# Stage 2's gate and value projections as seven products of quarters, with split weight quarters streamed from DRAM

## The chip, the core and the metric

The kernel runs on one core of one Trainium2 chip. The metric is device time in microseconds of one execution. The profile is one execution taken by the hardware profiler; it has its own time beside that of the runs.

## The reference

Three parts in a row, all in float32, over 2304 tokens (4 batches of 576) and a width of 512 (8 heads of 64):

```
attn = softmax(mask(q @ k.T / 8)) @ v          # window of 32; half of the heads with dilation 4
x1   = attn as (2304, 512)
x2   = ((x1 @ w1) * (x1 @ w2)) @ w3 @ w_out    # inner width 1024
out  = (silu(x2 @ w_gate) * (x2 @ w_val)) @ w_out2    # inner width 1536
```

## The kernel before

Everything is transposed: features lie on the 128 partitions and tokens along the free axis. The host only lays the inputs out. Weights come as 64-bit floats in blocks of two 128 x 512 pieces (`w_in`, 1 MB each), in the order of `W_ORDER` (lines 48 to 58).

A float32 product is made of three TensorE matmuls (`mm3`, lines 182 to 187): each operand is kept as a high part, rounded to the type `float32r`, and a low part, the rest, and high x high, high x low and low x high are summed in PSUM. `to_parts` (line 133) splits an operand: ScalarE copies it to the high part, VectorE subtracts. `convert_weights` (line 152) does it for a weight block: ScalarE and VectorE make a float32 of the 64-bit value (lines 166 to 170), ScalarE copies the high part (172), GpSimd subtracts (173).

Blocks of weights and of tokens pass through two or three staging buffers `raw`, in the order of the list `blocks` (line 95): `load_block` issues the DMA on SyncE's queue, `next_block` converts, `done_with` gives the buffer back and loads the next.

Stage 1 (lines 454 to 510) handles the tokens in four chunks of 512 and one of 256. For each of 8 inner blocks k it projects with `w1` (`gate_a`, 12 matmuls into bank `ba`), with `w2` (`gate_b`, 12 into `bb`), multiplies the two, splits the product `p`, and one block later contracts it with `w3 @ w_out`, made earlier on the chip (`contract`, 12 matmuls into four banks). The attention of the next batches runs between the blocks of chunks 0 to 2. In chunk 3 six of stage 2's weight blocks are converted, in chunk 4 nine.

Stage 2 (lines 513 to 537) does the same with 12 inner blocks, `Silu` on the gate, and all its weights resident in SBUF. Its x comes back from DRAM (`x2d`) a chunk at a time.

The program's order on each engine's queue is not the written one: the tile framework plans it from a timing model of its own, by readiness and the written order as priority. `tc.issue_after` ties instructions behind another on its engine.

Of the kernel before, what the change touches and what calls it, by code (L numbers as in the profile page):

```python
# [53 lines left out]
for _k in range(K2):  # L54
    W_ORDER.append((("wg", _k), ("wv", _k)))
    if _k % 2 == 0:
        W_ORDER.append((("wo2", _k), ("wo2", _k + 1)))
# [9 lines left out]
SPLIT_1 = {3: [1, 1, 1, 1, 1, 1, 0, 0], 4: [1, 1, 1, 1, 1, 1, 1, 2]}  # L67
SPLIT_2 = [1, 1, 1, 1, 0, 0, 0, 0, 0, 0, 0, 0]


def moe_chain_kernel(tc, q_in, k_in, v_in, w_in, mask_in, out):
# [8 lines left out]
    with static as st, other as ot, psum as pp, dram as dp:  # L80

        wslot = [st.tile([P, 2, 2, 512], F32R, name=f"w{i}") for i in range(12)]
        xb = [st.tile([P, 2, KT, CMAX], F32R, name=f"x{i}") for i in range(2)]
        pr = st.tile([P, 2, 2, CMAX], F32R, name="p")
        ta = st.tile([P, CMAX], F32, name="ta")
        raw = [ot.tile([P, 2, 512, 2], U32, name=f"raw{i}") for i in range(2)]
# [4 lines left out]
        x2d = dp.tile([KT, P, NT], F32, name="x2d")  # L91
        count = {"att": 0, "p": 0, "o": 0}


        blocks = [("w", i) for i in range(N_W1)] + [("x1", c) for c in (1, 2, 3)]
        blocks += [("w", i) for i in range(N_W1, N_W1 + 6)] + [("x1", 4)]
        blocks += [("w", i) for i in range(N_W1 + 6, N_W1 + 10)] + [("x2", 0)]
        blocks += [("w", i) for i in range(N_W1 + 10, NW)]
        blocks += [("x2", c) for c in range(1, NC)]
# [5 lines left out]

        def x_of(kind, c):
            return xb[(c + (NC if kind == "x2" else 0)) % 2]

        def load_block():
# [7 lines left out]
            if kind == "w":  # L117
                dst = r.rearrange("p (b f) -> p b f", b=2)
                src = w_in[i]
            else:  # L120
                a, size = CHUNKS[i]
                dst = r[:, :KT * size].rearrange("p (m t) -> p m t", m=KT)
                src = (x1d if kind == "x1" else x2d)[:, :, a:a + size].rearrange("m p t -> p m t")
# [3 lines left out]
        def done_with(n):  # L127

            if n < N_W1 or raw_at[n] is not raw[2]:
                raw_free.append(raw_at[n])  # L130
            load_block()
# [5 lines left out]
        def next_block():  # L137
# [5 lines left out]
            else:  # L143
# [3 lines left out]
                for m in range(0, KT, 2):  # L147
                    x = x_of(kind, i)[:, :, m:m + 2, :size]
                    to_parts(r[:, m:m + 2], x[:, 0], x[:, 1])
            done_with(n)  # L150

        def convert_weights(n, names):
# [10 lines left out]
            for b, w in slots:  # L163
                r = raw_at[n][:, b]
                lo, hi = r[:, :, :, 0], r[:, :, :, 1]
                nc.scalar.activation(hi.bitcast(F32), hi.bitcast(F32), AF.Prelu, scale=REBIAS, alpha=SIGN_UP)  # L166
                nc.vector.tensor_scalar(out=lo, in0=lo, scalar1=29, scalar2=None, op0=ALU.logical_shift_right)  # L167
                nc.vector.scalar_tensor_tensor(  # L168
                    out=lo, in0=hi, scalar=3, in1=lo, op0=ALU.logical_shift_left, op1=ALU.bitwise_or
                )  # L170
                x = lo.bitcast(F32)
                nc.scalar.activation(w[:, :, 0], x, AF.Copy)  # L172
                nc.gpsimd.tensor_tensor(out=w[:, :, 1], in0=x, in1=w[:, :, 0].bitcast(F32), op=ALU.subtract)  # L173

# [65 lines left out]
        with att1_pool as a1, att2_pool as a2:  # L240
# [5 lines left out]
            raw.append(a1.tile([P, 2, 512, 2], U32, name="raw2"))  # L246
            raw_free.extend(raw)
            xr = a1.tile([P, REST], F32, name="xr")
# [205 lines left out]
            def stage1(c, between, after):  # L454
                first, n = CHUNKS[c]
                x = x_of("x1", c)[:, :, :, :n]
# [19 lines left out]

            def rest(k):
# [13 lines left out]
        more1_pool = tc.tile_pool(name="more1", bufs=1, reuse_waits="tile")  # L491
        more2_pool = tc.tile_pool(name="more2", bufs=1, side="right", reuse_waits="tile")
        with more1_pool as m1, more2_pool as m2:
            assert not free and n_split[0] == N_W1 + 3
            free.extend([m1.tile([P, 2, 2, 512], F32R, name=f"wl{i}") for i in range(4)])
            free.extend([m2.tile([P, 2, 2, 512], F32R, name=f"wr{i}") for i in range(2)])

            def first_six(k):
                for _ in range(SPLIT_1[3][k]):
                    next_block_behind_p()  # L500
                if k == K1 - 1:
                    next_block()

            def replace(k):
                release(("w1", k), ("w2", k))
                for _ in range(SPLIT_1[4][k]):
                    next_block_behind_p()

            stage1(3, lambda n: None, first_six)
            stage1(4, lambda n: None, replace)  # L510


            for c, (first, n) in enumerate(CHUNKS):
                x = x_of("x2", c)[:, :, :, :n]
                for k in range(K2):
                    gate_a(("wg", k), x, n, AF.Silu)
                    p = gate_b(("wv", k), x, n)
                    flush()
                    if c == 0:
                        if k == 0:  # L520
# [83 lines left out]
```

## Time and profile before

| | us |
|---|---|
| three runs, median (lowest to highest) | 910.43 (908.68 to 911.29) |
| the profiled execution | 909.69 |
| its span, first to last instruction | 907.5 |
| TensorE busy | 881.4 |
| VectorE, ScalarE, GpSimd busy | 336.0, 312.3, 132.0 |

The profiled execution's time is 2.2 us more than its span; what lies outside is the start and the end of the program. Busy times of engines overlap, since engines run beside each other. A matmul's recorded time is its own latency, and the next one starts before it ends.

### The profile page before, as it was taken

To read this page: it belongs to the slowest core of one execution; us is meant where nothing else is said; L and a number is where in the kernel's file an instruction comes from. 1 tells how busy PE (TensorE), PEld (TensorE's weight loads), DVE (VectorE), ACT (ScalarE), POOL (GpSimd) and SP (SyncE) were. 2 spreads that over 40 slices of the span, in tenths; PEclk is the share of its full clock that TensorE was granted. 3 is DMA by queue.
4 is the path that set the end of the run, shared out by engine and by line. 5 is a ranking of instruction groups with operands and counts; after the bars stand their busy time and mean duration, and the time that the engine had idled before them with its cause. 6 is when DMAs were issued, how large, how long until landed. Compare 5 with 4: busy or idle time off the path is not lost.

```text
span 907.5 us, 11771 instructions
## 1 busy us (share of the span) xinstructions
PE 881.4 (97%) x4850; PEld 737.6 (81%) x4850; DVE 336.0 (37%) x487; ACT 312.3 (34%) x682; POOL 132.0 (15%) x83
## 2 busy tenths in 40 slices
PE   8889899989999999999999999999999999999998
PEld 5667688868888878889988888888888888888998
DVE  5887952333324213344766313111221112111221
ACT  4966743343525423343555212111221112111111
POOL 4656531000100100321343000000000000000000
PEclk8989899999999999999999999999999999999999
DMA  9786622332224113333555302000010001000100
GB/s 296 253 275 237 211 61 61 93 126 88 77 91 155 33 46 116 122 119 139 208 178 173 106 1 70 1 0 1 1 47 1 0 1 47 1 0 1 47 1 24
DMA packets 45909, 79.58 MB, mean 88 GB/s; under 512 B 3232, under 2 KB 29472, under 8 KB 41120
## 3 DMA queue, kind: packets, MB, share of 16 engines
q1 hardware_dynamic: 40096, 69.39, 23.5%
q10 hardware_dynamic: 5760, 9.44, 2.8%
q8 instruction: 38, 0.62, 0.3%
q14 instruction: 15, 0.12, 0.0%
HBM read 65.72 MB, written 13.11 MB: 87 GB/s over the span
## 4 chain that ended last, share of the span: by engine, by line
PE 83%; DVE 6%; DMA 4%; ACT 3%; issue 2%; POOL 1%; SPq 0%; DVEq 0%; POOLq 0%; ACTq 0%
PE bk L185 26%; PE bk L186 26%; PE bk L187 26%; PE bk L286 3%; DMA raw<-w_in 2%; DVE raw L168 2%; PE bk L338 2%; DVE raw L167 2%; PE bk L323 1%; POOL w L173 1%; ACT raw L166 1%; ACT s L305 1%; DMA q<-q_in 1%; ACT w L172 1%; DMA raw<-x1d 1%
## 5 line engine op out<-in xcount | busy, mean ns | idle before, releaser
L185 PE MATMUL bk<-x,w 128*128 128x512 f32 (+1 forms) x640 | 239.8, 375 | 3.2 <-ACT x L134 2.5
L186 PE MATMUL bk<-x,w 128*128 128x512 f32 (+1 forms) x640 | 238.5, 373 | 1.4 <-DVE x L135 1.4
L187 PE MATMUL bk<-x,w 128*128 128x512 f32 (+1 forms) x640 | 238.2, 372 | 0.0
L210 DVE TENSOR_TENSOR ta<-bk,ta 128x512 f32<-128x512 f32 (+1 forms) x100 | 63.7, 637 | 354.7 <-PE bk L187 323.7
L185 PEld LDWEIGHTS bk<-x,w 128*128 128x128 f32 x640 | 121.5, 190 | 23.5 <-ACT x L134 2.9
L186 PEld LDWEIGHTS bk<-x,w 128*128 128x128 f32 x640 | 121.6, 190 | 21.4 <-DVE x L135 2.4
L187 PEld LDWEIGHTS bk<-x,w 128*128 128x128 f32 x640 | 121.6, 190 | 19.8
L204 ACT ACTIVATE ta<-bk 128x512 f32<-128x512 f32 (+1 forms) x100 | 55.3, 553 | 227.2 <-PE bk L187 215.5
L186 PE MATMUL bk<-p,w 128*128 128x512 f32 (+1 forms) x320 | 118.5, 371 | 1.1 <-DVE p L135 1.1
L187 PE MATMUL bk<-p,w 128*128 128x512 f32 (+1 forms) x320 | 118.0, 370 | 0.0
L185 PE MATMUL bk<-p,w 128*128 128x512 f32 (+1 forms) x320 | 117.0, 371 | 0.0
L134 ACT ACTIVATE p<-ta 128x512 fp32r<-128x512 f32 (+1 forms) x100 | 58.7, 587 | 161.8 <-DVE ta L210 161.7
L135 DVE TENSOR_TENSOR p<-ta,p 128x512 fp32r<-128x512 f32 (+1 forms) x100 | 78.7, 787 | 55.3 <-ACT p L134 55.0
L173 POOL TENSOR_TENSOR w<-raw,w 128x1024 fp32r<-128x1024 f32 (+1 forms) x33 | 81.5, 2473 | 98.2 <-ACT w L172 98.2
L186 PEld LDWEIGHTS bk<-p,w 128*128 128x128 f32 x320 | 60.4, 189 | 11.6 <-DVE p L135 1.7
L187 PEld LDWEIGHTS bk<-p,w 128*128 128x128 f32 x320 | 60.4, 189 | 9.9
L185 PEld LDWEIGHTS bk<-p,w 128*128 128x128 f32 x320 | 59.8, 189 | 10.0 <-ACT p L134 0.2
L305 ACT ACTIVATE s<-s,sm 128x96 f32<-128x96 f32 x144 | 52.0, 363 | 41.3 <-DVE sm L303 41.2
L168 DVE SCALAR_TENSOR_TENSOR raw<-raw 128x1024 uint32<-128x1024 uint32 (+1 forms) x39 | 59.4, 1522 | 10.9 <-ACT raw L166 10.0
L310 POOL TENSOR_TENSOR s<-s,sm 128x480 f32<-128x480 f32 (+1 forms) x32 | 32.8, 1024 | 192.7 <-DVE sm L309 119.1
L166 ACT ACTIVATE raw<-raw 128x1024 f32<-128x1024 f32 (+1 forms) x39 | 43.8, 1124 | 30.1 <-DMA raw<-w_in 30.1
L172 ACT ACTIVATE w<-raw 128x1024 fp32r<-128x1024 f32 (+1 forms) x33 | 36.7, 1113 | 39.3 <-DVE raw L168 39.2
(80 smaller groups left out, 952.5 us busy)
## 6 DMA issues: line engine op xcount, KB each, us to landing
raw<-w_in SPq DMA_DIRECT2D x37, 1024.0 KB, 5.2
v<-v_in SPq DMA_DIRECT2D x16, 432.0 KB, 4.0
q<-q_in SPq DMA_DIRECT2D x32, 160.0 KB, 4.2
k<-k_in SPq DMA_DIRECT2D x16, 288.0 KB, 5.7
x2d<-o ACTq DMA_DIRECT2D x16, 256.0 KB, 2.0
raw<-x2d SPq DMA_DIRECT2D x4, 1024.0 KB, 5.2
out_t<-o ACTq DMA_DIRECT2D x16, 256.0 KB, 2.0
x1d<-o SPq DMA_DIRECT2D x12, 288.0 KB, 3.8
```

Of the source, the lines that this page charges most:

```text
L134: nc.scalar.activation(hi, src, AF.Copy)
L135: return nc.vector.tensor_tensor(out=lo, in0=src, in1=hi.bitcast(F32), op=ALU.subtract)
L166: nc.scalar.activation(hi.bitcast(F32), hi.bitcast(F32), AF.Prelu, scale=REBIAS, alpha=SIGN_UP)
L168: nc.vector.scalar_tensor_tensor(out=lo, in0=hi, scalar=3, in1=lo, op0=ALU.logical_shift_left, op1=ALU.bitwise_or)
L172: nc.scalar.activation(w[:, :, 0], x, AF.Copy)
L173: nc.gpsimd.tensor_tensor(out=w[:, :, 1], in0=x, in1=w[:, :, 0].bitcast(F32), op=ALU.subtract)
L185: nc.tensor.matmul(ps, wh, xh, start=start, stop=False)
L186: nc.tensor.matmul(ps, wh, xl, start=False, stop=False)
L187: nc.tensor.matmul(ps, wl, xh, start=False, stop=stop)
L204: nc.scalar.activation(ta[:, :n], ba[:, :n], func)
L210: nc.vector.tensor_tensor(out=u, in0=bb[:, :n], in1=ta[:, :n], op=ALU.mult)
L305: nc.scalar.activation(s[:, n], s[:, n], AF.Exp, bias=m[:, 0, n:n + 1], accum_out=m[:, 1, n:n + 1])
```

## The change

Stage 2's tokens go in three chunks of 768, each cut in two halves of 384 (`HT`). The inner blocks go in six pairs. For a pair, the gate (or value) projection is a product of a 2 x 2 array of weight quarters (two inner blocks by two halves of the 512 inputs) with a 2 x 2 array of x quarters (two halves of the inputs by two halves of the tokens), which takes 7 products of quarters in place of 8, by Strassen's scheme in Winograd's form: four sums of weight quarters (`S1` to `S4`), four sums of x quarters, and sums of the results.

- Weight sums are made and split in stage 1's chunks 1 to 3, six blocks in each, and written to DRAM (`wd`, `wod`). One staging buffer (`raw[2]`) goes after chunk 0, and its place is taken by two buffers for what goes out.
- In stage 2 the split quarters come back through a ring of 14 buffers, one DMA of 0.5 MB for each of 126 products; `wo2` comes twice a step.
- The x operands of a chunk, seven of 2 x 384 columns with a high and a low part, are made in stage 1's chunk 4 for the first and in the last step of the chunk before for the others.
- Results are summed by VectorE as they come (`evacuate`). The contraction with `wo2` goes in units of six matmuls between the products of the next step, and VectorE adds them up in SBUF (`oacc`).

The diff, cut to its core:

```diff
+FP = K2 // 2
+TOK = 768
+HT = TOK // 2
+NC2 = NT // TOK
+S1, S2, S4, S3, A11, A12, A22 = range(7)
+SPOT = [A11, S2, A12, S1, S3, S4, A22]
+BANK = [0, 1, 2, 0, 1, 2, 0]
+NOP = 9
+NRING = 14
+UNITS = [1, 1, 1, 1, 1, 1, 2]
...
+            def quarters():
...
+                x = to_float32(raw_at[n])
+                yield
+                if kind != "wo2":
...
+                    add = nc.vector.tensor_tensor
+                    add(out=t[S1], in0=b[:, 1, 0], in1=b[:, 1, 1], op=ALU.add)
+                    add(out=t[S3], in0=b[:, 0, 0], in1=b[:, 1, 0], op=ALU.subtract)
+                    add(out=t[S2], in0=t[S1], in1=b[:, 0, 0], op=ALU.subtract)
+                    add(out=t[S4], in0=b[:, 0, 1], in1=t[S2], op=ALU.subtract)
+                    yield
+                for i in range(2):
+                    stage = stages[n_stage[0] % 2]
...
+                        split_to(w[:, :4], sums[:, :, f])
+                        split_to(w[:, A11:A11 + 2], b[:, 0, :, f])
+                        split_to(w[:, A22:A22 + 1], b[:, 1, 1:2, f])
+                        dst, src = wd[j, :, :, m, i], stage.rearrange("p (s f) -> p s f", s=7)
+                    nc.sync.dma_start(out=dst.bitcast(F32), in_=src.bitcast(F32))
+                    yield
...
+                done_with(n)
...
             def rest(k):
...
+                if n_split[0] > N_W1:
+                    if k == 0:
+                        work.extend([quarters() for _ in range(6)])
+                    step(99 if k == K1 - 1 else 3)
                 if k == K1 - 1:
                     next_block()
...
+                for r, of in enumerate([
+                    lambda: b11, lambda: less(t2, b22, less(t1, b12, b11)), lambda: b21, lambda: t1,
+                    lambda: less(t1, b22, b12), lambda: b22, lambda: less(t2, b21, t2),
+                ]):
+                    src = of()
+                    o = operand(c, r)
+                    to_parts(src, o[:, 0], o[:, 1])
+                    if r < 6:
+                        yield
...
+            def fill(upto=7 * FP * NC2):
+                while n_ring[0] < min(n_used[0] + len(ring), upto):
...
+                    nc.sync.dma_start(out=dst.rearrange("p b s h f -> p b s (h f)").bitcast(F32), in_=wd[j, :, SPOT[r]].bitcast(F32))
...
+            banks = [[batt[0], ba, acc[0]], [batt[1], bb, acc[1]]]
+            cbank = [b[:, :HT] for b in acc[2:]]
...
+            def product(c, j, r):
+                w, x = ring[n_used[0] % len(ring)], operand(c, r)
+                for m in range(2):
+                    ps = banks[m][BANK[r]][:, :HT]
+                    for kt in range(2):
+                        mm3(ps, (w[:, m, kt, 0], w[:, m, kt, 1]), (x[:, 0, kt], x[:, 1, kt]), kt == 0, kt == 1)
...
+                def add(dst, x, y):
+                    for m in range(2):
+                        nc.vector.tensor_tensor(out=dst[m], in0=x[m], in1=y[m], op=ALU.add)
+                def gated(u, h, i):
+                    nc.scalar.activation(u[0], u[0], AF.Silu)
+                    nc.vector.tensor_tensor(out=u[1], in0=u[1], in1=u[0], op=ALU.mult)
+                    to_parts(u[1], p[h][i][:, 0], p[h][i][:, 1])
+                if r == 0:
+                    for m in range(2):
+                        nc.scalar.activation(a[m], ps[m], AF.Copy)
+                elif r == 1:
+                    add(b, ps, a)
+                elif r == 2:
+                    add(a, ps, a)
+                    gated(a, 0, 0)
+                elif r == 3:
+                    add(d, ps, b)
+                elif r == 4:
+                    add(b, ps, b)
+                    add(a, kept, b)
+                    gated(a, 1, 1)
+                elif r == 5:
+                    add(d, ps, d)
+                    gated(d, 1, 0)
+                else:
+                    add(b, ps, b)
+                    gated(b, 0, 1)
...
+                        def unit(h=h, m=m):
...
+                            for i in range(2):
+                                w = wo[i]
+                                mm3(ps, (w[:, 0, cs], w[:, 1, cs]), (p[h][i][:, 0], p[h][i][:, 1]), i == 0, i == 1)
+                            a = oacc[:, m, h * HT:(h + 1) * HT]
+                            if j == 0:
+                                nc.vector.tensor_copy(a, ps)
+                            else:
+                                nc.vector.tensor_tensor(out=a, in0=ps, in1=a, op=ALU.add)
+                            if j == FP - 1:
+                                t = c * TOK + h * HT
+                                nc.sync.dma_start(out=out[m * P:(m + 1) * P, t:t + HT], in_=a)
...
+            for n in range(FP * NC2):
+                c, j = divmod(n, FP)
+                if j == FP - 1 and c + 1 < NC2:
+                    work.append(operands())
+                    step(2)
+                for r in range(7):
+                    product(c, j, r)
+                    if n == 0 and r == 1:
+                        flush_first()
...
+                    evacuate(r, p)
+                    fill()
+                    contract_some(UNITS[r])
+                    step()
```

## Rows read from the trace of the kernel before

**Rows 1.** The page: busy time by engine; PE and its granted clock in 40 slices.

```profile
PE 881.4 (97%) x4850; PEld 737.6 (81%) x4850; DVE 336.0 (37%) x487; ACT 312.3 (34%) x682; POOL 132.0 (15%) x83
...
PE   8889899989999999999999999999999999999998
...
PEclk8989899999999999999999999999999999999999
```

**Rows 2.** The page's chain that ended last, by line.

```profile
PE bk L185 26%; PE bk L186 26%; PE bk L187 26%; PE bk L286 3%; DMA raw<-w_in 2%; DVE raw L168 2%; PE bk L338 2%; DVE raw L167 2%; PE bk L323 1%; POOL w L173 1%; ACT raw L166 1%; ACT s L305 1%; DMA q<-q_in 1%; ACT w L172 1%; DMA raw<-x1d 1%
```

**Rows 3.** Windows, stage 1's chunks 1, 3, 4, stage 2: PE PEld DVE ACT POOL, clock, DMA, GB/s.

```profile
185.60:269.20 83.60, 81.14 (x513) 66.18 (x512) 24.91 (x51) 31.85 (x98) 7.81 (x8) 0.98 0.29 92
...
352.70:418.25 65.55, 65.55 (x291) 54.28 (x290) 24.27 (x32) 25.44 (x33) 14.62 (x6) 1.00 0.34 121
418.25:455.46 37.21, 36.11 (x290) 35.42 (x288) 24.98 (x30) 16.16 (x27) 9.85 (x4) 1.00 0.49 170
455.46:903.50 448.04, 446.91 (x2174) 377.80 (x2172) 113.86 (x155) 99.06 (x157) 19.51 (x8) 1.00 0.10 33
```

**Rows 4.** Timeline of PE where stage 2 begins: start us, us, instruction, [idle before].

```profile
460.93 0.28 PE L185 MATMUL bk<-p,w 128*128 128x256 f32 x1
...
...
463.64 0.50 PE L185 MATMUL bk<-x,wl 128*128 128x512 f32 x1 [1.12 <-ACT ta L204]
```

**Rows 5.** Timeline in stage 2: 512 columns, weight loads, then 256 columns.

```profile
840.73 0.39 PE L185 MATMUL bk<-x,w 128*128 128x512 f32 x1
840.73 0.19 PEld L186 LDWEIGHTS bk<-x,w 128*128 128x128 f32 x1
...
846.17 0.39 PE L185 MATMUL bk<-p,w 128*128 128x512 f32 x1
...
847.83 0.69 DVE L135 TENSOR_TENSOR p<-ta,p 128x512 fp32r<-128x512 f32 x1 [0.70 <-ACT p L134]
...
848.89 0.28 PE L185 MATMUL bk<-x,wl 128*128 128x256 f32 x1
...
851.76 0.40 PE L185 MATMUL bk<-p,w 128*128 128x512 f32 x1
```

**Rows 6.** Lines, shapes apart: out<-in, count | busy us, mean ns | idle before.

```profile
L300 DVE SCALAR_TENSOR_TENSOR s<-bk,mask 128x384 f32<-128x384 f32 x24 | 13.2, 551 | 5.3 <-PE bk L286 5.3
...
L172 ACT ACTIVATE w<-raw 128x1024 fp32r<-128x1024 f32 x31 | 35.4, 1142 | 37.1 <-DVE raw L168 37.0
...
L325 ACT ACTIVATE pt<-bk 96x384 f32<-96x384 f32 x48 | 22.4, 480 | 30.7 <-PE bk L323 28.4 <-PE bk L187 1.6 <-ACT o L227 0.4
...
L173 POOL TENSOR_TENSOR w<-raw,w 128x1024 fp32r<-128x1024 f32 x31 | 78.9, 2550 | 93.7 <-ACT w L172 93.7
```

**Rows 7.** Timeline of DVE and POOL in stage 1's chunk 4.

```profile
422.64 0.69 DVE L167 TENSOR_SCALAR raw<-raw 128x1024 uint32<-128x1024 uint32 x1
423.24 0.69 DVE L229 COPY o<-bk 128x512 f32<-128x512 f32 x1
423.84 1.22 DVE L168 SCALAR_TENSOR_TENSOR raw<-raw 128x1024 uint32<-128x1024 uint32 x1
...
444.08 0.42 DVE L135 TENSOR_TENSOR p<-ta,p 128x256 fp32r<-128x256 f32 x1
...
432.47 2.48 POOL L173 TENSOR_TENSOR w<-raw,w 128x1024 fp32r<-128x1024 f32 x1 [3.40 <-ACT w L172]
...
432.73 2.50 DVE L135 TENSOR_TENSOR p<-ta,p 128x256 fp32r<-128x256 f32 x1 [0.97 <-ACT p L134]
```

**Rows 8.** Timeline of PE at the last contraction.

```profile
901.88 0.64 PE L185 MATMUL bk<-p,w 128*128 128x256 f32 x4
```

**Rows 9.** Windows of 20 us with much DMA, columns as in rows 3.

```profile
20.00:40.00 20.00, 16.30 (x147) 12.59 (x146) 16.61 (x27) 17.17 (x52) 11.02 (x9) 1.00 0.91 302
480.00:500.00 20.00, 20.00 (x88) 16.27 (x87) 13.14 (x13) 10.42 (x12) 8.78 (x4) 1.00 0.50 174
```

**Rows 10.** DMA issues: out<-in, queue, count, KB each, median us to landing.

```profile
raw<-x1d SPq DMA_DIRECT2D x3, 1024.0 KB, 5.2
```

More of the change, by code (lines that the diff above doesn't have):

```diff
@@ L53 @@
 N_W1 = len(W_ORDER)
[L54 to L57, printed above, removed]
+for _k in range(0, K2, 2):
+    W_ORDER += [(("wg", _k), ("wg", _k + 1)), (("wv", _k), ("wv", _k + 1)), (("wo2", _k), ("wo2", _k + 1))]
 NW = len(W_ORDER)
@@ L91, in moe_chain_kernel @@
         x2d = dp.tile([KT, P, NT], F32, name="x2d")
+        wd = dp.tile([FP, P, 7, 2, 2, 2 * P], F32R, name="wd")
+        wod = dp.tile([FP, P, 2, 2 * 512], F32R, name="wod")
         count = {"att": 0, "p": 0, "o": 0}
[L95 to L99, printed above, removed]
+        blocks = [("w", i) for i in range(N_W1)] + [("x1", 1)]
+        for c in (1, 2, 3):
+            blocks += [("w", i) for i in range(N_W1 + 6 * (c - 1), N_W1 + 6 * c)] + [("x1", c + 1)]
+        blocks += [("x2", (c, j)) for c in range(NC2) for j in range(2)]
         n_loaded, n_split = [0], [0]
@@ L127, in done_with @@
         def done_with(n):
-            if n < N_W1 or raw_at[n] is not raw[2]:
+            if n < N_W1 - 3 or raw_at[n] is not raw[2]:
                 raw_free.append(raw_at[n])
@@ L147, in next_block @@
                 for m in range(0, KT, 2):
[L148 removed]
+                    x = xb[i % 2][:, :, m:m + 2, :size]
                     to_parts(r[:, m:m + 2], x[:, 0], x[:, 1])
@@ L455, in stage1 @@
                 first, n = CHUNKS[c]
-                x = x_of("x1", c)[:, :, :, :n]
+                x = xb[c % 2][:, :, :, :n]
                 for k in range(K1):
@@ L477, in rest, with step @@
+            def step(n=1):
+                while n and work:
+                    try:
+                        with tc.issue_after(last_p[0]):
+                            next(work[0])
+                        n -= 1
+                    except StopIteration:
+                        work.popleft()
             def rest(k):
@@ L488, in moe_chain_kernel @@
                 stage1(c, attend_in(c), rest)
[L491 to L502, printed above, removed]
-            def replace(k):
[L505 to L509, printed above, removed]
-            stage1(4, lambda n: None, replace)
[L513 to L520, printed above, removed]
-                            free.extend(wslot[8:])
-                        for _ in range(SPLIT_2[k]):
-                            next_block_behind_p()
-                    if k == 8 and c + 1 < NC:
-                        next_block()
-                    def fin(c=c, k=k, p=p, first=first, n=n):
-                        contract(slot_of["wo2", k], p, n, k == 0, k == K2 - 1)
-                        if k == K2 - 1:
-                            bufs = None
-                            if c == NC - 1:
-                                r = raw[0].rearrange("p b f w -> p (b f w)").bitcast(F32)
-                                bufs = [r[:, m * n:(m + 1) * n] for m in range(KT)]
-                            drain(lambda m: out[m * P:(m + 1) * P, first:first + n], n, bufs)
-                    pend.append(fin)
-            flush()
@@ new lines, in moe_chain_kernel @@
+                if c == 0:
+                    raw_pool.__exit__(None, None, None)
+                    stage_pool = tc.tile_pool(name="stages", bufs=1)
+                    sp = stage_pool.__enter__()
+                    stages.extend(sp.tile([P, 1792], F32R, name=f"stage{i}") for i in range(2))
+            stage_pool.__exit__(None, None, None)
+        mid_pool = tc.tile_pool(name="mid", bufs=1, side="right", reuse_waits="tile")
+        late_pool = tc.tile_pool(name="late", bufs=1, reuse_waits="tile")
@@ L540, in mask_of @@
+        late_pool.__exit__(None, None, None)
 def mask_of():
```

155 lines of the change are left out of this document (135 added, 20 removed).

## The prediction

> **What bounds the kernel now.** I read the page first. TensorE (PE) is busy 97% of the span, the next engine (VectorE, DVE) 37%, and in the 40 slices PE is at 9 tenths from the tenth slice to the last but one, its granted clock at 9 from the sixth [rows 1]. The chain of waits says the same: 78% of it is the three matmul lines of `mm3` [rows 2]. So a second is won or lost where PE columns are, or where something makes PE wait.
>
> Then the table by stage [rows 3]. Stage 1's chunks 1 to 4 run 185.6 to 455.46, stage 2 from 455.46 to the end of the last matmul, 448.0 us, with PE busy for all but 1.1 us, DVE for 114, ScalarE (ACT) for 99 and DMA at a tenth. Inside it lie stage 1's last contraction (12 matmuls of 256 columns from 460.93, 1.4 us) and the gap behind it, 1.3 us up to 463.64, where PE waits for ACT's first Silu [rows 4]. 448.0 - 1.4 - 1.3 = 445.3 us is stage 2 proper: 4 chunks x 12 x 36 = 1728 matmuls of 512 columns and 432 of 256.
>
> What one matmul costs is the distance between starts, not the recorded 0.39 or 0.28 us, which overlap. 24 matmuls of 256 columns lie between 848.89 and 851.76: 0.120 us each. 24 of 512 lie between 840.73 and 846.17: 0.227 us [rows 5]. Over the whole stage the 512s cost (445.3 - 432 x 0.120) / 1728 = 0.2277 us, since some stretches run a little wider; I use that.
>
> **The change, part by part.**
>
> *Products.* Per pair step (two gate blocks, two value blocks, 768 tokens) 7 products of 2 x 2 x 3 = 12 matmuls of 384 columns stand for 8; the contraction has 8 units of 6. That is 132 matmuls x 18 steps = 2376, in place of 2160. No row has 384 columns. From the line through 256 and 512, a matmul costs (0.120 + 0.2277) / 2 = 0.1738 us. Bounds: 0.160 (the line's slope alone, 384 x 0.42 ns, with no fixed part) and 0.190, the weight load's recorded time, if it were a floor [rows 5]; I take the line, because 0.120 at 256 columns already undercuts that floor, and both lengths carry the same 13 ns beyond the slope. 2376 x 0.1738 = 413.0, so PE's own need falls by 445.3 - 413.0 = 32.3 us: 34.6 from an eighth of the projections' columns, less 216 more matmuls at a fixed 13 ns or so.
>
> A weight load starts at 840.73 beside a running matmul and costs PE nothing [rows 5]. The Trainium skill, "TensorE: Matmul & The Clock Gate", section "The mechanism", says that a weight load overlaps matmuls in flight only if its row group differs; all loads here fill the same rows, so by it each of the 216 added matmuls would also pay a load. By the rows they don't, and by the rule the gain would shrink by 216 x 0.19 = 41 us and be gone.
>
> *Evacuation.* Before, a k step costs DVE 2 operations and ACT 2. After, a pair step has 14 sums, 4 products, 4 subtractions and 8 accumulations: 30 DVE operations of 384 columns, and 10 on ACT. A two-input DVE operation of 384 columns from PSUM took 0.551 us, an ACT copy of that length 0.480 [rows 6]. Neighbours on DVE overlap: one recorded at 0.69 is followed 0.60 later [rows 7]. So 0.46 each, 30 x 0.46 = 13.8 us of DVE beside 132 x 0.1738 = 22.9 us of PE. ACT needs under 5. On average DVE hides (60%), with three places where it is close:
> - In the last step of chunks 0 and 1 the next chunk's seven operands are made: 11 DVE operations of 768 columns, between 0.69 (512) and 1.22 (1024) [rows 7], some 0.87 in a row; 9.6 us more makes 23.4 against 22.9. If DVE also sits out each ACT round trip (0.70 [rows 5] for each of 4 halves, about 0.8 for each of 7 operands) it needs 23.4 + 2.8 + 5.6 = 31.8, and PE loses 8.9 twice.
> - Products 6 and 0 use bank 0 one after the other; the cover is two units, 2.1 us, against two sums and the hand-over, some 1.5 us. If DVE is late by half a us, 18 x 0.5 = 9 us.
> - Step 0 has no contraction to cover it, and the last unit is exposed: 0 to 5 us.
>
> Together 0 to 18 + 9 + 5 = 32, if every engine keeps the written order. It does not: the order on each queue is planned, and the trace shows pieces pulled forward: four first matmuls of the last contraction ahead of the second and third ones that wait for DVE [rows 8], a copy put between two halves of a conversion [rows 7]. With three pairs of banks PE can take a later product instead of waiting. I take 4 us.
>
> *Streaming.* Before, stage 2's weights are resident. Now 126 ring loads of 0.52 MB, 36 of `wo2` halves, 6 x blocks and the outputs make 66.1 + 18.9 + 4.7 + 4.7 = 94 MB in 413 us, 229 GB/s. The 20 us window 20:40 moved 302 GB/s at a DMA share of 0.91 [rows 9]. So 70% of what is shown, on the same queue, with 14 slots (some 45 us) of lead: I cost it at nothing. SP's order is load, load, then an output that waits for DVE; the lead covers that.
>
> *Stage 1, chunks 1 to 3.* Conversions of stage 2's weights move forward from chunks 3 and 4 and stage 2, and grow: a gate or value block gets 4 DVE sums of 256 columns (0.42 each), ACT splits 2 x 896 columns in six pieces for 1024 in one (some 2.6 us for 1.14), POOL the same (4.4 us for 2.55) [rows 6], and two stores to DRAM that queue on SP behind POOL's result, with the next block's load behind them. Per chunk (4 such blocks, 2 of `wo2`): ACT 4 x 3.75 + 2 x 2.3 = 19.6, DVE 4 x 3.6 + 2 x 1.9 = 18.2, POOL 22.6, stores 9.4 MB. In chunk 1 that lifts ACT from 31.9 to 51, DVE from 24.9 to 43, POOL from 7.8 to 30 of 83.6 us [rows 3]. Chunk 3, which had six conversions before, had no PE gap at all, so the work itself hides. Two things may not: a DVE subtraction of 256 columns took 2.50 us instead of 0.42 while POOL ran [rows 7], and each x chunk is now loaded only when the fifth block of six has left its buffer (there are two, not three), so at three chunk ends the load (5.2 us [rows 10]) and its conversion (4 us) may come after PE's last matmul. Bounds: 0, and 3 x 4 us for the ends plus some 8 for blocked subtractions, 20. I take 4.
>
> On POOL's grip the Trainium skill, "SBUF — State Buffer", section "SBUF: two separate sides", says that a DVE operation with two SBUF inputs and a GpSimd operation exclude each other for a whole instruction. By it the 48 new sums can be held up as well, at most for POOL's 17.6 us in a chunk: DVE would then be busy 61 of 83.6 us, still less than PE; the row shows this for the subtraction alone.
>
> *What goes.* In chunk 4 nine conversions go and one operand set (7 operands) comes; PE lost 1.1 us of 37.2 there and 1.1 at the table load [rows 3, 4]. The first gap goes (-1.1); the second I leave.
>
> *Tail.* As before: a last evacuation and a store of about 2 us.
>
> **Sum.** Span 907.5 plus 2.2 around it = 909.7, the profiled execution (0.7 under the median of 910.4). 909.7 - 32.3 + 4 (evacuation) + 4 (stage 1) - 1.1 = 884.3; 884.
>
> **Rivals.**
> - *DVE's order stalls PE*: PE waits for banks in every step, and DVE sets the pace where operands are made. For: single sum buffers, bank 0 twice in a row, 12 dependent hand-overs a step. Against: DVE at 60%, order planned. Stage 2 gives back up to 32 in place of 4: centre 24, 904.
> - *Stage 1 does not hide the bigger conversions*: 20 in place of 4: 900.
> - *The stream starves the ring* (slower): PE waits for ring loads. It decides where less than 94 MB / (413 + 25) = 215 GB/s are delivered; below that the gain is gone. The nearest row of a steady mix under full compute moved 174 GB/s [rows 9], though at a share of 0.50, that is, unasked for more. At 174 stage 2 takes 94 / 0.174 = 540 us: 909.7 - 445.3 + 540 + 3 = 1007; at 205 GB/s 459 us: 926. For: 9 loads a step on one queue, each waiting for PE. Against: 302 in rows.
> - *The pitch does not follow the columns* (slower): at a floor of 0.190 a matmul, 451 us, 909.7 + 6 + 7 = 923. The 256-column rows contradict it. The Trainium skill's rule on weight loads, above, would lead to a similar place.
> - *The projections don't shrink*: excluded by counting, 84 matmuls for 96 in a step at equal columns.
>
> **How the numbers follow.** The forecast 0.68 (874 to 893), DVE order 0.14 (893 to 908), stage 1 0.07 (893 to 902), starvation 0.07, pitch 0.04. Low end: no stall anywhere, 909.7 - 32.3 - 2.4 = 875, less one for the narrower 512 pitch carried over: 873. High end 904 leaves the slower cases and a quarter of the order case out, under 2 in 10. 0.3% is 2.7 us, about what a measurement here can tell from no change: slower 0.11, within it 0.03 (the end of the order case), faster 0.86.
>
> **What would show it.** Right: starts of 384-column matmuls 0.173 to 0.175 us apart; 1512 + 864 of them; stage 2 between 413 and 422 us with DVE at 60 to 70%; chunks 1 to 3 each within 3 us of before. Wrong: PE idle before a product released by DVE or ACT (order), by a DMA into the ring (starvation), by the x conversion at a chunk end (stage 1), or a pitch at 0.19. A DVE above 85% in stage 2 would tell that 0.46 is too low. I would be wrong outright if stage 2 took more than 440 us.

## The result and the profile after

The changed kernel takes 894.83 us (median of four runs, 892.81 to 895.88) against 910.45 before on the same chip: ratio 0.9828, interval 0.9806 to 0.9851. The gain is 15.6 us where 26 were forecast. The profiled execution took 895.88, the longest of the four and 1 us above their median; its span is 894.1.

The page after: busy time, PE and its granted clock in 40 slices, and the chain that ended last, by line.

```profile
PE 859.2 (96%) x5065; PEld 780.3 (87%) x5066; DVE 567.2 (63%) x968; ACT 351.4 (39%) x809; POOL 166.8 (19%) x149
...
PE   8889899999998989899899999999999999999998
...
PEclk9999799999999999899999999999999999999999
...
PE bk L210 20%; PE bk L211 20%; PE bk L212 20%; DMA raw<-w_in 8%; DMA raw<-x1d 3%; POOL stage L508 3%; DVE raw L195 2%; PE bk L312 2%; DMA wd<-mid 2%; DMA wd<-stage 1%; ACT raw L193 1%; DMA x1d<-o 1%; ACT s L331 1%; DVE raw L194 1%; PE bk L364 1%
```

Against [rows 1], 8s have appeared in PE's row in the 13th, 15th, 17th and 20th slices. Against [rows 2], the three matmul lines (now 210 to 212) hold 60% of the chain, not 78%: in the first half it now runs through the x load from DRAM (`raw<-x1d`), the weight loads, the quarter stores (`wd<-stage`) and POOL. From stage 2 on it is 98% matmuls.

Windows after, columns as in [rows 3]: from the x conversion at the end of chunk 0 to chunk 4's first matmul; chunk 4 with stage 2; the same from the first 384-column matmuls on; then the first microseconds after the gaps at the ends of chunks 1, 2 and 3.

```profile
185.62:435.42 249.80, 235.93 (x1330) 190.94 (x1330) 128.29 (x203) 124.46 (x309) 92.44 (x98) 0.97 0.76 248
...
435.43:891.00 455.57, 454.49 (x2676) 452.69 (x2676) 320.53 (x596) 120.03 (x224) 0.00 (x0) 1.00 0.63 207
...
446.76:890.60 443.84, 443.39 (x2612) 442.51 (x2610) 316.43 (x588) 116.53 (x217) 0.00 (x0) 1.00 0.62 204
...
276.50:279.90 3.40, 3.37 (x10) 2.64 (x11) 3.39 (x5) 3.40 (x14) 0.00 (x0) 0.52 1.05 297
362.65:368.60 5.95, 5.91 (x13) 4.22 (x14) 2.94 (x3) 2.58 (x3) 0.00 (x0) 0.50 0.97 342
435.40:439.90 4.50, 4.25 (x19) 3.66 (x20) 1.90 (x3) 1.01 (x2) 0.00 (x0) 0.68 0.88 295
```

The same first stretch in the kernel before:

```profile
186.69:418.25 231.56, 229.93 (x1331) 188.55 (x1331) 78.25 (x133) 90.12 (x223) 27.36 (x20) 0.99 0.29 98
```

By the two profiled executions, with the forecast beside them:

| stretch | before | after | difference | forecast |
|---|---|---|---|---|
| to chunk 0's end | 186.7 | 185.6 | -1.1 | 0 |
| chunks 1 to 3, to chunk 4's first matmul | 231.6 | 249.8 | +18.2 | +4 |
| chunk 4 and stage 2, to the last matmul's end | 485.2 | 455.2 | -30.1 | -29.4 |
| tail | 4.0 | 3.5 | -0.5 | 0 |
| span | 907.5 | 894.1 | -13.4 | -25.4 |

So stage 2 came out as forecast, and stage 1 lost 14 us more than it was allowed. In chunks 1 to 3 PE's idle time went from 231.56 - 229.93 = 1.6 us to 13.9, and the same matmuls were busy 6.0 us longer. Most of both stands at the ends of the chunks. The timeline of PE after, at the ends of chunks 1, 2 and 3 (start, us, instruction, idle before and what ended it):

```profile
276.53 1.17 PE L210 MATMUL bk<-x,w 128*128 128x512 f32 x2 [2.29 <-ACT x L157]
...
362.65 1.22 PE L210 MATMUL bk<-x,w 128*128 128x512 f32 x2 [3.42 <-ACT x L157]
...
364.51 0.63 PE L212 MATMUL bk<-x,w 128*128 128x512 f32 x1
364.93 0.63 PE L210 MATMUL bk<-x,w 128*128 128x512 f32 x1
...
435.42 0.39 PE L210 MATMUL bk<-x,w 128*128 128x256 f32 x1 [3.56 <-ACT x L157]
```

At the end of chunk 2 PE idles for 3.42 us, until ACT has converted x for the next chunk. The matmuls behind the gap start 0.42 us apart (364.51, 364.93), not 0.227: the granted clock is 0.50 of full speed for 6 us, the level of 1.2 GHz. At the end of chunk 1 PE idles for 2.29 us, with a clock of 0.52 behind it, and at that of chunk 3 for 3.56 us, with 0.68: 9.3 us of waiting for x in all. Behind chunk 0's end the clock is low in both kernels (0.63 over 4.4 us after, 0.69 before).

Why x is late, on the other queues at chunk 2's end (`SPq` is a DMA issued by SyncE, `x1d` is attention's output in DRAM, `wd` the stored quarters):

```profile
343.82 0.33 SPq L390 DMA_DIRECT2D x1d<-o  x1
...
349.76 1.79 SPq L545 DMA_DIRECT2D wd<-stage  x2
351.73 1.32 SPq L148 DMA_DIRECT2D raw<-x1d  x1
...
361.55 2.00 ACT L157 ACTIVATE x<-raw 128x1024 fp32r<-128x1024 f32 x2 [2.47 <-DMA raw<-x1d]
```

Attention's last store to `x1d` is issued at 343.82, the x load 7.9 us later, just behind two quarter stores: `x` has to have the staging buffer of the block that these finish. It has landed when ACT starts at 361.55, 9.8 us on; PE ran dry at 359.2. At chunk 1's end the wait is another one. The chain that ended last reads there

```profile
261.67 7.44 DMA x1d<-o
...
269.12 6.28 DMA raw<-x1d
```

The x load is issued as soon as attention's store has landed, but that took 7.44 us, where the kernel before needed 3.5.

### The profile page after: what moved, and what is told of

It is laid out like the page before. It is cut to its first block, busy times and chain, and to the rows that moved or that the text cites. A ratio compares the mean times of both kernels' runs of the same rounds, so it can differ in the third digit from the quotient of the medians.

```text
span 894.1 us, 13459 instructions
## 1 busy us (share of the span) xinstructions
PE 859.2 (96%) x5065; PEld 780.3 (87%) x5066; DVE 567.2 (63%) x968; ACT 351.4 (39%) x809; POOL 166.8 (19%) x149
## 4 chain that ended last, share of the span: by engine, by line
PE 64%; DMA 17%; ACT 5%; DVE 5%; POOL 4%; issue 3%; SPq 1%; ACTq 0%; POOLq 0%; DVEq 0%
PE bk L210 20%; PE bk L211 20%; PE bk L212 20%; DMA raw<-w_in 8%; DMA raw<-x1d 3%; POOL stage L508 3%; DVE raw L195 2%; PE bk L312 2%; DMA wd<-mid 2%; DMA wd<-stage 1%; ACT raw L193 1%; DMA x1d<-o 1%; ACT s L331 1%; DVE raw L194 1%; PE bk L364 1%
## 5 line engine op out<-in xcount | busy, mean ns | idle before, releaser
L695 DVE TENSOR_TENSOR s<-bk,s 128x384 f32<-128x384 f32 x252 | 137.5, 554 | 48.9 <-PE bk L212 28.5
L210 PE MATMUL bk<-x,w 128*128 128x512 f32 (+2 forms) x368 | 139.7, 382 | 11.5 <-ACT x L157 11.3
L211 PE MATMUL bk<-x,w 128*128 128x512 f32 (+2 forms) x368 | 139.4, 379 | 1.7 <-DVE x L158 1.6
L212 PE MATMUL bk<-x,w 128*128 128x512 f32 (+2 forms) x368 | 138.3, 376 | 0.0
L212 PE MATMUL bk<-p,wo 128*128 128x384 f32 x288 | 97.3, 338 | 0.0
L210 PE MATMUL bk<-p,wo 128*128 128x384 f32 x288 | 96.8, 337 | 0.0
L211 PE MATMUL bk<-p,wo 128*128 128x384 f32 x288 | 96.8, 336 | 0.0
L737 DVE TENSOR_TENSOR acc<-bk,acc 128x384 f32<-128x384 f32 x120 | 66.5, 554 | 43.9 <-PE bk L212 43.5
L210 PEld LDWEIGHTS bk<-x,w 128*128 128x128 f32 x368 | 71.6, 196 | 23.7 <-ACT x L157 12.8
L698 ACT ACTIVATE s<-s 128x384 f32<-128x384 f32 x72 | 37.8, 526 | 129.6 <-DVE s L695 128.5
L211 PEld LDWEIGHTS bk<-x,w 128*128 128x128 f32 x368 | 71.5, 194 | 13.1 <-DVE x L158 3.5
L212 PEld LDWEIGHTS bk<-x,w 128*128 128x128 f32 x368 | 71.7, 195 | 9.9
L235 DVE TENSOR_TENSOR ta<-bk,ta 128x512 f32<-128x512 f32 (+1 forms) x40 | 25.4, 636 | 75.2 <-PE bk L212 47.6
L210 PE MATMUL bk<-w 128*128 128x384 f32 (+1 forms) x196 | 70.3, 366 | 2.3 <-ACT w L188 2.0
L211 PE MATMUL bk<-w 128*128 128x384 f32 (+1 forms) x196 | 69.7, 360 | 0.5 <-POOL w L189 0.5
L211 PE MATMUL bk<-w,mid 128*128 128x384 f32 x204 | 68.6, 336 | 0.0
L212 PE MATMUL bk<-w,mid 128*128 128x384 f32 x204 | 67.9, 337 | 0.0
L210 PE MATMUL bk<-w,mid 128*128 128x384 f32 x204 | 67.8, 336 | 0.0
L212 PE MATMUL bk<-w 128*128 128x384 f32 (+1 forms) x196 | 67.4, 356 | 0.0
L508 POOL TENSOR_TENSOR stage<-raw,stage 128x512 fp32r<-128x512 f32 (+2 forms) x56 | 52.4, 962 | 75.2 <-ACT stage L507 75.2
```

Of the source, the lines that this page charges most:

```text
L210: nc.tensor.matmul(ps, wh, xh, start=start, stop=False)
L211: nc.tensor.matmul(ps, wh, xl, start=False, stop=False)
L212: nc.tensor.matmul(ps, wl, xh, start=False, stop=stop)
L235: nc.vector.tensor_tensor(out=u, in0=bb[:, :n], in1=ta[:, :n], op=ALU.mult)
L508: nc.gpsimd.tensor_tensor(out=dst[:, :, 1], in0=src, in1=dst[:, :, 0].bitcast(F32), op=ALU.subtract)
L695: nc.vector.tensor_tensor(out=dst[m], in0=x[m], in1=y[m], op=ALU.add)
```

## The experiments

Theory A: the x chunk waits for a staging buffer that a quarter block holds, and the gap costs in two ways, as idle time and as matmuls at 1.2 GHz. Theory B: the stores of the quarters delay it, by their place on SP's queue or by their bytes. Theory C: ACT, DVE and POOL are simply too full. For stage 2 two questions stood: whether the stream really is free, and whether the planned order is what hides the evacuation. Edits are against the changed kernel unless they say otherwise; "the stretch" is that of chunks 1 to 3 in the table above (249.8 us). In the three kernels that leave stage 1 as it is (the lone stream, the short lead, the written order) it took 245.0, 246.8 and 246.8, so less than 5 us in it, from one profiled execution, means nothing. A ratio is to the kernel before, run beside it on the same chip; that kernel's medians lay between 910.4 and 911.8.

**x loaded straight into its tile.** The raw x goes into the low half of its own operand tile as soon as attention has stored it, and is split in place; no staging buffer.

```diff
-    blocks += [("w", i) for i in ...] + [("x1", c + 1)]
+    blocks += [("w", i) for i in ...]
...
+    dst = xb[c % 2][:, 1, :, :size]
+    nc.sync.dma_start(out=dst.bitcast(F32), in_=x1d[:, :, a:a + size].rearrange("m p t -> p m t"))
...
+    hi, lo = x1_parts(c + 1, m)
+    to_parts(lo.bitcast(F32), hi, lo)
```

> The x chunks 2, 3 and 4 are loaded straight into the low half of their own tile, as soon as attention has written them, and split there; no staging buffer is needed. Theory A (x comes late because its load waits for a staging buffer, behind the fifth of six weight blocks): PE's waits for x at the ends of chunks 1, 2 and 3 (2.6, 3.6 and 3.7 us) go, and with them the half-clock matmuls behind them (1.6, 3.0 and 1.2 us): 12 to 16 us less than the changed kernel's 894.8, 879 to 883. Theory B (x comes late because its DMA shares the queue and the engines with the stores of the quarters): the load still lands late, 889 or more. Theory C (ScalarE and VectorE are too full of quarter work to split x in time): no change, 893 to 896.

886.54 us (885.09 to 887.97), ratio 0.9732, interval 0.9707 to 0.9757: 8.3 us below the changed kernel, and the fastest version of this study, but short of the 12 to 16 us that theory A expected. The stretch took 237.3. Windows (the stretch, and the microseconds behind chunk 1's end), then PE's wait for x in the stretch (total us, times, longest):

```profile
186.62:423.91 237.29, 230.00 (x1331) 187.64 (x1332) 129.04 (x204) 124.18 (x308) 91.17 (x97) 1.00 0.79 258
...
277.30:283.00 5.70, 4.98 (x21) 3.81 (x22) 2.90 (x5) 4.93 (x15) 0.83 (x1) 1.00 0.93 314
```

```profile
PE bk L210 <- ACT x L157: 4.0, 2, 2.3
```

PE's waits for x in the changed kernel, and in the one before, each over its own stretch:

```profile
PE bk L210 <- ACT x L157: 10.8, 4, 3.6
```

```profile
PE bk L185 <- ACT x L134: 1.9, 1, 1.9
```

Of 10.8 us of waiting for x, 4.0 are left: 1.7 at chunk 0's end, where the kernel before waited 1.9, and 2.3 at chunk 1's. Busy time is back at the old 230.0, with the clock at 1.00, behind these two gaps as well. In the changed kernel the clock fell behind gaps of the same lengths (1.6 and 2.29 us), so the length of a gap alone does not tell whether it falls, and why it did not here is not shown. The timeline at chunk 2's end, with SP's queue:

```profile
342.13 0.34 SPq L390 DMA_DIRECT2D x1d<-o  x1
345.69 0.38 SPq L572 DMA_DIRECT2D x<-x1d  x1
...
348.99 0.39 PE L212 MATMUL bk<-p,W 128*128 128x512 f32 x1
349.22 0.39 PE L210 MATMUL bk<-x,w 128*128 128x512 f32 x1
```

The load now follows the store by 3.6 us, as long as that takes to land, and the next chunk starts 0.23 us after the last contraction. Theory A holds for the ends of chunks 2 and 3, where no wait for x is left. At chunk 1's end PE still waits 2.3 us; there the same view reads

```profile
260.75 2.75 SPq L390 DMA_DIRECT2D x1d<-o  x1
...
269.62 0.38 SPq L572 DMA_DIRECT2D x<-x1d  x1
...
276.39 1.06 ACT L157 ACTIVATE x<-x 128x1024 fp32r<-128x1024 f32 x1 [0.91 <-DMA x<-x1d]
```

and in the kernel before

```profile
258.93 0.33 SPq L364 DMA_DIRECT2D x1d<-o  x1
...
262.51 0.38 SPq L125 DMA_DIRECT2D raw<-x1d  x1
```

Before, store to load took 3.6 us there; now 8.9, and ACT has x only 6.8 us after the load's issue. No staging buffer is in that path any more: what is left at chunk 1's end is not theory A's.

**Quarter work drawn sooner** (four pieces a step, not three), so that the buffer comes free earlier:

```diff
-    step(99 if k == K1 - 1 else 3)
+    step(99 if k == K1 - 1 else 4)
```

> Four steps of quarter work per inner block in place of three, so that the six blocks of a chunk are done two inner blocks before its end, and the staging buffer for x comes free earlier; nothing else changes. Theory A: most of the same gain, 881 to 887, limited by when attention has written x. Theory B: the stores crowd the earlier part, and x lands later than its buffer would allow, 887 to 893. Theory C: denser work on VectorE, ScalarE and GpSimd makes PE wait inside the chunks, 895 or more.

898.49 us (895.66 to 901.58), ratio 0.9866, 0.9828 to 0.9903: no faster, the answer that stood for theory C. Yet x does come sooner. PE's waits for x in the stretch:

```profile
PE bk L210 <- ACT x L157: 5.5, 2, 3.7
```

Two of the four waits are gone, those at the ends of chunks 2 and 3, as theory A has it for these. The gain is lost in other places: the wait at chunk 1's end grows from 2.3 to 3.7 us, PE waits 5.2 us for ACT inside the chunks, not 2.7, and 2.8 more at stage 2's start, with a clock of 0.65 behind it; chunk 4 and stage 2 take 3.7 us longer than in the changed kernel.

**A seventh of the quarters' bytes stored** (the ring reads part 0):

```diff
-    dst, src = wd[j, :, :, m, i], stage.rearrange("p (s f) -> p s f", s=7)
+    dst, src = wd[j, :, :1, m, i], stage.rearrange("p (s f) -> p s f", s=7)[:, :1]
...
-    in_=wd[j, :, SPOT[r]]
+    in_=wd[j, :, 0]
```

> The changed kernel (894.8) with one of the seven parts of each weight store (left out: the other six; the ring reads the first part every time). The queue's order and the staging buffers are as in the changed kernel, only the stored bytes fall from 9.4 to some 3 MB a chunk. If the bytes of the stores are what makes x and the staging buffers late (B2): stage 1 gets 10 us or more shorter, 880 to 885. If it is the order of buffers and queue (A, B1): 888 to 895.

887.91 us in one run, the stretch 241.2. A store (KB, median us from issue to landing), the stretch's window, and two of PE's waits in it:

```profile
wd<-stage SPq DMA_DIRECT2D x16, 128.0 KB, 1.7
```

```profile
188.00:429.19 241.19, 232.07 (x1330) 189.08 (x1331) 128.10 (x202) 122.16 (x309) 92.95 (x98) 0.98 0.56 179
```

```profile
PE bk L349 <- ACT pt L351: 4.9, 1, 4.9
PE bk L210 <- ACT x L157: 3.3, 2, 1.8
```

The store with all bytes, in the changed kernel, and what ACT waits there for such stores in the stretch:

```profile
wd<-stage SPq DMA_DIRECT2D x16, 896.0 KB, 6.6
```

```profile
ACT stage L507 <- DMA wd<-stage: 22.7, 10, 5.3
```

6.9 us come back, between the two answers expected, while DVE, ACT and POOL do as much as ever (128, 122, 93 us): against theory C as the reason why x is late. The waits for x at the ends of chunks 2 and 3 are gone here too, with the staging buffers as they were. The bytes act by way of the buffers: a copy into a `stage` buffer has to wait until the store that last used it has landed, which keeps the block's staging buffer, and no such wait is left with the short stores. So theories A and B are two ends of one chain. What is left is at chunk 1's end, mostly a wait of 4.9 us for attention (`pt`).

**Both at once**: the direct load, with this on top.

```diff
-    dst, src = wd[j, :, :, m, i], stage.rearrange("p (s f) -> p s f", s=7)
+    dst, src = wd[j, :, :1, m, i], stage.rearrange("p (s f) -> p s f", s=7)[:, :1]
```

> Both cuts at once: x straight into its own tile, and one of the seven parts of each weight store (left out: the other six). Alone they took stage 1's chunk 4 start from 435.4 to 423.9 and to 429.2. If they are two causes that add up (a late buffer and crowded transfers), chunk 4 starts at 417 to 420 and the whole takes 879 to 883, stage 1 as before the change. If one cause is behind both: no earlier than 423, 885 to 888.

888.05 us in one run, the stretch 239.2: nothing on top of the direct load, as it should be if both act on one wait. Chunk 1's end is no better: x's load is issued 7.7 us after attention's store (266.08 and 273.81 on SP's queue).

**Other queues**, on top of the direct load: the quarters' stores, and then x's store and load, issued by GpSimd.

```diff
-    nc.sync.dma_start(out=dst.bitcast(F32), in_=src.bitcast(F32))
+    nc.gpsimd.dma_start(out=dst.bitcast(F32), in_=src.bitcast(F32))
```

> On top of the kernel that loads x into its own tile (886.5): the stores of the quarters are issued on GpSimd's queue, right behind the subtraction whose result they carry, in place of SyncE's. At the end of chunk 1 of that kernel PE still waited for x, and SyncE's queue held x's load behind a store that waits for GpSimd. Theory B1 (the order on SyncE's queue holds x back): the remaining wait for x goes, 3 to 5 us less, 881 to 884. Theory B2 (the transfers themselves are slow, because stores, loads of weights and x share the 16 engines): same time, 885 to 888. Against both: issuing costs GpSimd time or is slower from there, 889 or more.

914.35 us (911.35 to 918.24), ratio 1.0032, 1.001 to 1.0054: the whole gain gone; the stretch 259.4, 22 us above the direct load's. Lines and DMA issues:

```profile
L545 POOL DMA_DIRECT2D wd<-stage x16 | 15.3, 990 | 1.5 <-POOL stage L508 1.5
...
wd<-stage POOLq DMA_DIRECT2D x16, 896.0 KB, 9.8
```

A store occupies POOL for 0.99 us, among its subtractions, and lands after 9.8 us, not the 6.3 of the kernel that this one is built on.

```diff
-    nc.sync.dma_start(out=x1d[hp, :, b * S:(b + 1) * S], in_=o)
+    nc.gpsimd.dma_start(out=x1d[hp, :, b * S:(b + 1) * S], in_=o)
...
-    nc.sync.dma_start(out=dst.bitcast(F32), in_=x1d[...])
+    nc.gpsimd.dma_start(out=dst.bitcast(F32), in_=x1d[...])
```

> On top of the same kernel (886.5): attention's stores of x and the loads of x chunks 2 to 4 are issued on GpSimd's queue, so that they don't stand behind the quarters' stores on SyncE's; the quarters' stores stay where they were. Theory B1 (queue order): x arrives some 4 us earlier at the end of chunk 1, 881 to 885. Theory B2 (shared transfer): 885 to 888. GpSimd waits in order for x's store to land before it can go on with the quarters: if that hurts, 889 or more.

905.25 us (901.91 to 906.57), ratio 0.9945, 0.9925 to 0.9966; the stretch 255.7. DMA issues, and POOL's wait:

```profile
x<-x1d POOLq DMA_DIRECT2D x2, 1024.0 KB, 11.5
```

```profile
POOL x1d L390 <- DVE o L389: 36.3, 5, 10.9
```

The issue waits on POOL for attention's output, up to 10.9 us, with the quarters' subtractions queued behind it. PE's waits for x are 2.9 us in two, against 4.0 in the direct load, but it now waits 8.4 us for attention's `pt`. Leaving SP's queue costs more than it can bring; what the order on that queue costs by itself neither run shows.

**Attention sooner, all x direct, and less work in chunk 1**, each on top of the direct load: attention spread over 0.6 of a chunk's matmuls instead of 0.75; chunk 1's x loaded in the same way as the others; 5, 6 and 7 quarter blocks in chunks 1 to 3 in place of 6 each.

```diff
-ATT_BY = 0.75
+ATT_BY = 0.6
```

> x straight into its own tile (886.5) and attention done at 0.6 of a chunk in place of 0.75, so that its last result is stored, and x loaded, one inner block (10 us) earlier. If x's path (store, then load, beside the quarters' stores) is what PE still waits for at the end of chunk 1: 2 to 4 us less, 882 to 885. If attention packed closer costs PE waits of its own: 888 or more.

898.34 us (895.77 to 899.54), ratio 0.9871, 0.9854 to 0.9889: worse. PE now waits inside attention (over the whole span; 6.7 in the direct load):

```profile
PE bk L364 <- ACT pt L351: 9.6, 5, 3.3
```

```diff
-blocks = [("w", i) for i in range(N_W1)] + [("x1", 1)]
+blocks = [("w", i) for i in range(N_W1)]
...
-x1_loaded = {1}
+x1_loaded = set()
```

> x straight into its own tile (886.5) for chunk 1 as well. PE waits about 2.5 us for x at the end of chunk 0, before the change too. If a late buffer is behind that as well: 1 to 3 us less, 883 to 886. If it is attention's store that is late there: no change, 885 to 888.

887.11 us (886.6 to 892.62), ratio 0.9757, 0.9726 to 0.9789: no difference from the direct load alone, so no late buffer is behind chunk 0's end.

```diff
-    work.extend([quarters() for _ in range(6)])
-    step(99 if k == K1 - 1 else 3)
+    work.extend([quarters() for _ in range(n_quarters[c])])   # [0, 5, 6, 7]
+    step(99 if k == K1 - 1 else 4 if c == 3 else 3)
```

> x straight into its own tile (886.5), and five, six and seven blocks of quarter work in chunks 1, 2 and 3 in place of six each (four steps an inner block in chunk 3, which has no attention). In chunk 1 the work then ends one inner block earlier, and its last stores and loads are off the DMA engines when x is stored and loaded. If that crowding is what is left at the end of chunk 1: 2 to 5 us less, 881 to 885. If it is something else there: 885 to 888. If chunk 3 can't hold seven blocks: 889 or more.

888.98 us (888.07 to 889.78), ratio 0.9755, 0.9736 to 0.9774: no gain. In chunk 1, x's load still comes 8.5 us after its store (272.33 against 263.81). The DMA engines' share in these 8.5 us is 1.07, as full as with six blocks, so this run did not take away the crowding that it was to test.

**Stage 2 without its stream**: only the first 14 of 126 ring loads.

```diff
-    nc.sync.dma_start(out=dst..., in_=wd[j, :, SPOT[r]]...)
+    if n_ring[0] < len(ring):
+        nc.sync.dma_start(out=dst..., in_=wd[j, :, SPOT[r]]...)
```

> Left out: all but the first 14 of the 126 ring loads (the products read what lies in the ring), 59 MB less from DRAM in stage 2. If the stream is hidden, as the prediction had it, stage 2 keeps its time: its 384-column matmuls stay 0.174 us apart and the whole is within 2 us of 894.8. If the ring loads hold PE up or slow its reads, stage 2 gets shorter by 5 us or more.

**A lead of 3 ring loads** instead of 14.

```diff
-    while n_ring[0] < min(n_used[0] + len(ring), upto):
+    while n_ring[0] < min(n_used[0] + 3, upto):
```

> The changed kernel (894.8) with a lead of 3 ring loads in place of 14. The stream was hidden with 14. A load took about 4.3 us from issue to landing, and a product with its unit takes 3.1 us, so 3 ahead (9 us) should just do: 893 to 900 if only latency counts. If the loads queue behind wo2's and x's on the same queue, PE waits for DMA in some steps: 905 or more.

893.0 and 893.54 us in one run each, both as expected of a hidden stream. Chunk 4 and stage 2, first without the stream, then with the short lead:

```profile
433.10:887.70 454.60, 454.23 (x2676) 452.77 (x2676) 320.65 (x595) 120.06 (x224) 0.00 (x0) 1.00 0.23 78
```

```profile
432.70:888.30 455.60, 455.39 (x2676) 453.64 (x2676) 320.25 (x596) 119.91 (x224) 0.00 (x0) 0.99 0.64 207
```

454.6 us at 78 GB/s and 455.6 at 207, as in the changed kernel: between these profiles the stream costs 1 us, and a lead of 3 is enough.

**Stage 2 in the written order**: its PE, DVE and ACT instructions are pinned to program order.

```diff
+    def keep(ins):
+        return tc.keep_in_program_order(ins) if pinned[0] else ins
...
-    nc.tensor.matmul(ps, wh, xh, start=start, stop=False)
+    keep(nc.tensor.matmul(ps, wh, xh, start=start, stop=False))
...
+    pinned[0] = True
     for n in range(FP * NC2):
```

> Every matmul, VectorE and ScalarE instruction of stage 2's loop is kept in the written order on its engine; nothing else changes. The prediction had 4 us of stalls because the order is planned, and 24 (up to 32) in the written order. If that is the reason, stage 2 grows by 15 to 30 us, to 910 to 925 in all, with PE waits on VectorE at bank 0 and in the two steps that make operands. If the order doesn't matter (VectorE at two thirds is enough by itself): 893 to 898.

928.51 us in one run, above the 910 to 925 expected. Windows (chunk 4 and stage 2; step 0; some steady steps; the two stretches that make operands), and the longest of PE's waits:

```profile
434.48:923.20 488.72, 468.03 (x2676) 459.11 (x2676) 317.17 (x595) 119.62 (x224) 0.00 (x0) 0.97 0.61 193
...
470.00:500.00 30.00, 24.37 (x137) 23.41 (x136) 12.67 (x26) 8.99 (x17) 0.00 (x0) 0.90 0.78 277
500.00:590.00 90.00, 90.00 (x512) 89.09 (x511) 59.73 (x116) 18.83 (x38) 0.00 (x0) 1.00 0.64 194
590.00:625.00 35.00, 28.63 (x150) 27.17 (x149) 27.09 (x46) 11.88 (x20) 0.00 (x0) 0.90 0.64 210
...
735.00:775.00 40.00, 33.65 (x173) 32.21 (x172) 29.44 (x51) 13.27 (x23) 0.00 (x0) 0.91 0.54 169
```

```profile
PE bk L215 <- DVE acc L742: 10.8, 6, 4.7
```

488.7 us against 455.6: 33 more. PE idles for 488.7 - 468.0 = 20.7 us, 19.6 more than in the changed kernel, and is busy 13.5 longer, as the clock falls to 0.90 in the stretches with waits. The idling is in the range expected; the clock's part was not in it. Two of the three places that the prediction named hold the idling, step 0 and the stretches that make operands (6 us in each of the three windows); the third, bank 0 in every step, does not: the steady steps lose nothing even in the written order.

## Why the prediction was right in stage 2 and wrong in stage 1

894.8 lies in the stated range, but above 893, where the forecast's own part of it ended. What carried it there is the rival on stage 1, to which 0.07 had been given; the high end of 904 had been set for another rival, DVE's order, which did not come. That the number still fell into the range is in part luck.

- *Pitch.* Right. Timeline of PE in stage 2, after:

```profile
700.52 0.33 PE L210 MATMUL bk<-w,x 128*128 128x384 f32 x1
...
702.08 0.34 PE L211 MATMUL bk<-w,mid 128*128 128x384 f32 x1
```

Nine intervals in 1.56 us are 0.173 each. Over the stage: of the 2612 matmuls from 446.76 on, 236 have 256 columns, 28.3 us at 0.120; the other 2376 take 443.84 - 28.3 = 415.5 us, 0.175 each, against 413.0 forecast: 2.5 us more. A weight load still lies beside every one (442.51 us of PEld in that window), so the rule on row groups of the Trainium skill ("TensorE: Matmul & The Clock Gate", section "The mechanism") does not hold for these loads: by it 41 us would have been lost. The same section also lets a load into the array's background weight buffer be pulled ahead of matmuls in flight; whether these loads go there no view shows.
- *Evacuation.* The 4 us were not needed: PE is idle for 0.45 us of 443.84. The recorded duration was as read from the rows (0.554 against 0.551), but taking 0.46 of it, for overlap with the neighbour, was too low: 252 sums were busy for 137.5 us, 0.55 each, and DVE is at 316 / 444 = 71%, where the sum had 60%. It hid all the same:

```profile
L695 DVE TENSOR_TENSOR s<-bk,s 128x384 f32<-128x384 f32 x252 | 137.5, 554 | 48.9 <-PE bk L212 28.5 <-ACT s L704 18.5
```

  The reason given, that the order is planned, is what the written order shows: PE idles 19.6 us more with it. That stage 2 then grew by 33, beside the rival's bound of 32, is chance. The bound was 18 where operands are made, 9 at bank 0 and 5 in step 0, all of it idling; the windows show 12.7, nothing and 5.6, and 13.5 us of slower matmuls that the bound did not have. Pitch and stalls together: -32.3 + 4 = -28.3 forecast, 415.5 - 445.3 = -29.8 measured; two misses of opposite sign stand behind that.
- *Streaming at nothing.* Right, within the 1 us between the two profiles.
- *Chunk 4, -1.1.* Its own gap went, but it now starts behind 3.56 us of idling with 4.5 us at a clock of 0.68: 455.2 - 415.5 = 39.7 us against 485.2 - 445.3 = 39.9.
- *Stage 1 at +4.* This is the step that failed: a term of the sum that was mis-sized, 4 for a measured 18 (13 to 18 by the spread of the stretch). Its three allowances of 4 us for x at the chunk ends came near their whole price, 2.3 + 3.4 + 3.6 = 9.3 of 12 us. At the ends of chunks 2 and 3 the reason is the one that was named, the x load behind the fifth block, which is late because its copies wait for stores that take 6.6 us to land, on a DMA load of 248 GB/s where the kernel before moved 98. At chunk 1's end it is attention's own store, 7.44 us in place of 3.5, which was not named. The matmuls behind the gaps ran at 1.2 GHz: of the 6.0 us by which matmuls were busy longer, 0.48 x 3.40 + 0.50 x 5.95 = 4.6 are in the two stretches shown, and the sum had no such term. The remaining 3 us are small waits, most of them for attention. The other item of the list, DVE blocked by POOL, cost PE next to nothing: it waited 0.2 us for a subtraction of `p`, and the 48 sums of 256 columns took 0.42 to 0.56 us on the mean of their lines. So the bounds (0 to 20) held the 18 in part by luck, since 8 of the 20 were for that item and none for the clock. "Chunks 1 to 3 each within 3 us of before" was wrong, 18 us in three. Taking 4 rested on chunk 3 of the kernel before, which had as many conversions and no gap; but that kernel had a third buffer, and stored nothing.

What stays open: 5.7 us of the 18 remain with the direct load (237.3 against 231.6), 2.3 of it at chunk 1's end, the rest in small waits for attention and operands. At chunk 1's end attention's store takes 7.4 to 9.4 us to land in every variant that leaves it on SP's queue, against 3.5 before. The DMA engines' share in that time is 0.92 to 1.07 in the five variants for which it was read, against 0.48 before. Fewer stored bytes, earlier attention and less work in chunk 1 did not change that, so that crowded transfers are the cause fits but is not shown. Nor is it shown why the clock fell behind some short gaps and not behind others.

## What to carry to other kernels

A load that is moved behind other work should be priced at the moment when its data are needed: which buffer it must have, what still holds that, and when the holder's own store lands. Where the final tile is free, load into it and split in place. And allow for up to as much again behind a gap of some us in front of matmuls, where the rows show a lower clock behind such gaps; work that is hidden on the average may still sit in the chain at a boundary.

## What was not expected of the hardware

After PE had idled 3.42 us, matmuls of 512 columns started 0.42 us apart instead of 0.227, at a granted clock of 0.50, for 6 us: the gap cost about 6.4 in all (5.95 us at half the clock is some 3 us of work at the full one). Shorter gaps went either way: behind 1.6 and 2.29 us the clock was 0.63 and 0.52 in the changed kernel, behind 1.7 and 2.3 us in the direct load it stayed at 1.00. Large DMAs issued by GpSimd were slower to land than the same ones from SyncE (9.8 us against 6.3 for a quarter store of 0.9 MB, 11.5 against 5.9 for 1 MB of x), and the store took 0.99 us of the engine; attention's stores of 288 KB were not slower (3.8 against 3.9). Ring loads at 207 GB/s beside a TensorE that never idles cost it nothing that could be measured.
